# Second phase's x: 32x32 blocks turned by VectorE and a DRAM scratch read back by columns, in place of TensorE transposes

## The chip, the core and the metric

The kernel runs on one core of a Trainium2 chip. The metric is device time in microseconds (us) of one execution. A core has five engines that each work through their own instructions in order and wait for one another by semaphores: TensorE (PE in the profile; PEld is its weight load), VectorE (DVE), ScalarE (ACT), GpSimd (POOL) and SyncE (SP), which here issues all the DMAs ("SPq" is its queue).

## What is computed

An mLSTM attention block, then two MoE-like feed-forward layers, one after the other, on 3072 tokens of width 320 with an inner width of 2048, all in float32:

```
x = attn_out.transpose(0, 2, 1, 3).reshape(B * S, H * D)   # 3072 x 320
x = _moe_ref(x, ...)       # h = x @ w_in; g = h * clip(h + 3, 0, 6) / 6; g @ w_out
return _moe2_ref(x, ...)   # h = x @ w_in; g = max(h, 0) ** 2;           g @ w_out
```

The attention runs in chunks of 64 steps for 4 batches of 768 steps. The change touches only what lies between the first layer's output and the second layer's input.

## The kernel before

**Tiling.** The 3072 tokens are cut into six blocks `j` of 512: 128 steps of each of the 4 batches `i`. `X[j]` is one tile of 128 partitions (the steps) by 4 batches by 320 features. It holds the attention's output, then the first layer's output, then the second layer's, each written over the one before. A layer (`ph` 0 or 1, the first and second phase) works through each block in 16 slots `m`, one for each 128 of the 2048 inner features. Slots are counted through both phases: in phase 0 block 0 has 24 (its first half goes in two halves), every other block 16, so 104 in phase 0 and 96 in phase 1.

**One slot.** `mm_A` (L634) multiplies w_in by x: 8 matmuls into the PSUM tile `hps`. The operand is `xs[ph, j]`, a tile of x turned so that features lie on the partitions, split into a high part (fp32r, entries 0 to 2) and a low part (entries 3, 4 and the upper half of 2). `act1` (ACT) and `act1b` (DVE) make g from it, `act2` (mostly ACT) and `act2b` (DVE) split g into `gh` and `gl`. `mm_B` (L673) multiplies by w_out: 3 matmuls for each batch, added up over the 16 slots of a block in four PSUM tiles `acc0` to `acc3`, of which there is one each. `mm_B` runs LAG = 2 slots behind `mm_A`.

**Between the blocks.** Behind the last slot of a block, `evac` (L685) empties the four `acc` tiles into `X[j]`; in phase 0 four ACT instructions do this (L688) and scale by 1/6. The next block's first `mm_B` writes the same `acc` tiles, so it waits for `evac`. Before a block starts, its x has to be turned: `t_pe` (L609) makes three TensorE transposes of 128x128 for one batch into a PSUM tile `tp`; `t_hi` (L618, usually ACT) copies `tp` into the high part, and `t_lo` (L622, DVE, two instructions, L625 and L627) makes the low part. For phase 1 these three steps stand in slots 13, 10, 7 and 4 ahead of the block, one batch each.

**What sets the order.** All instructions are written out by hand. `FIRST` is a list of steps that run first, with an engine behind "@" where it isn't the usual one; it reaches through the first 40 slots, block 0's `evac` among them. Behind it stand the steps of `moe()`: for every slot `mm_A`, `act1`, `act1b`, the steps hooked at "pe", `mm_B` of two slots ago, `evac`, the steps hooked at "ew" (attention, loads, weight work), `act2`, `act2b`. The attention units are hooked into phase 0 up to slot 84, and the second layer's weights are loaded and split (`w_load`, `w_exp`, `w_bits`, `w_hilo`) from slot 90 on, since they lie in the same SBUF as the first layer's.

Of the kernel before, what the change touches and what calls it, by code (L numbers as in the profile page):

```python
# [8 lines left out]
F32 = mybir.dt.float32  # L9
F32R = mybir.dt.float32r  # L10
# [3 lines left out]
ACTF = mybir.ActivationFunctionType  # L14
ALU = mybir.AluOpType
# [12 lines left out]
TB = 512  # L28
# [93 lines left out]
def kernel(ctx, tc, qk, kn, va, gates, og, w1i, w1o, w2i, w2o, out):  # L122
    nc = tc.nc
    B, NC, D, _, H, _ = qk.shape
    BH = B * H
    S = NC * L
    NT, DM = out.shape
    NG, P, KI3, GC = w1i.shape
    MG = w1o.shape[2]
    NM = NG * MG  # L130
    E0 = 64
    KX = E0 + D
    DV = D + 1
    NPR = S // P
# [16 lines left out]
    xs_p = ctx.enter_context(tc.tile_pool(name="xs", bufs=2))  # L151
    g_p = ctx.enter_context(tc.tile_pool(name="g", bufs=2))
    gh_p = ctx.enter_context(tc.tile_pool(name="gh", bufs=3))
    at2 = ctx.enter_context(tc.tile_pool(name="at2", bufs=2))
    dram = ctx.enter_context(tc.tile_pool(name="dram", bufs=1, space=DRAM))
# [13 lines left out]
    kI = [const.tile([KX, H, D], F32, name=f"kI{i}") for i in range(3)]  # L169
    Z = [[const.tile([KX, H, DV], F32, name=f"Z{b}{i}") for i in range(2)] for b in range(B)]  # L170
    X = [xpool.tile([P, B, DM], F32, name=f"X{p}") for p in range(NPR)]
    Gd = dram.tile([NC, BH, L], F32, name="Gd")

    UL = 4
# [8 lines left out]
    for step in FIRST.split():  # L183
        step, _, eng = step.partition("@")
        if eng:
            name, _, a = step.partition(":")
            ENG[(name, *(int(n) for n in a.split(",")))] = eng

    def on(name, usual, *a):
        return {"v": nc.vector, "g": nc.gpsimd}[ENG.get((name, *a), usual)]  # L190

    def copy(name, *a):
        return nc.vector.tensor_copy if ENG.get((name, *a)) == "v" else nc.scalar.copy
# [13 lines left out]
    gb = pre[:, B, 0:NC1 * P].rearrange("p (c k) -> p c k", k=P)  # L207
    gx, gy = (t[0:BH].rearrange("p b d -> p (b d)") for t in X[NPR - 2:])

# [117 lines left out]
    T = {}  # L327
# [77 lines left out]
    def x_tile(u):  # L405
        if ("X", u) not in T:
            T["X", u] = at2.tile([KX, H, KX], F32, tag="Xm", name="Xm")
        return T["X", u]

# [73 lines left out]
    def at_Y(u):  # L483
        b, c = units[u]
        Xm = T["X", u]
        pool, tag = (ps_acc, "acc0") if u in (1, 3) else (ps_y, "y")
# [41 lines left out]
    def at_n3(u):  # L528
        b, c = units[u]
        yt = T["yt", u]  # L530
        p0 = (c % 2) * L
        xo = X[c // 2][p0:p0 + L, b, :].rearrange("p (h d) -> p h d", d=D)
        on("at_n3", "v", u).tensor_tensor(out=xo, in0=xo, in1=yt[p0:p0 + L], op=ALU.mult)  # L533
# [72 lines left out]
    xs = {}  # L606


    def t_pe(ph, j, i):  # L609
        x = X[j][:, i, :]  # L610
        if (ph, j) not in xs:
            xs[ph, j] = xs_p.tile([P, 5, TB], F32R, tag="xs", name="xs")
        tp = T["tp", ph, j, i] = ps_s.tile([P, 3, P], F32, tag="s", name="tp")

        for k, c0 in enumerate((0, P, KB)):
            nc.tensor.transpose(out=tp[:, k, :], in_=x[:, c0:c0 + P], identity=ident)  # L616

    def t_hi(ph, j, i):  # L618
        n = slice(i * P, i * P + P)
        copy("t_hi", ph, j, i)(out=xs[ph, j][:, 0:3, n], in_=T["tp", ph, j, i])  # L620

    def t_lo(ph, j, i):  # L622
        t, tp = xs[ph, j], T["tp", ph, j, i]
        n = slice(i * P, i * P + P)
        nc.vector.tensor_tensor(  # L625
            out=t[:, 3:5, n], in0=tp[:, 0:2], in1=t[:, 0:2, n].bitcast(F32), op=ALU.subtract)
        nc.vector.tensor_tensor(  # L627
            out=t[0:E0, 2, n], in0=tp[E0:P, 2], in1=t[E0:P, 2, n].bitcast(F32), op=ALU.subtract)

    acc = {}  # L630
# [54 lines left out]
    def evac(s, i):  # L685
        ph, j, m, i0, i1 = slots[s]
        if ph == 0:
            nc.scalar.activation(out=X[j][:, i, :], in_=acc[i], func=ACTF.Copy, scale=1.0 / 6.0)  # L688
        else:
            copy("evac", s, i)(out=X[j][:, i, :], in_=acc[i])  # L690
            r0 = i * S + j * P
            nc.sync.dma_start(out=out[r0:r0 + P, :], in_=X[j][:, i, :])
# [9 lines left out]
    first = {}  # L702
# [8 lines left out]
    at_x2 = (x_q, x_k)  # L711
    at_norm = (at_n1, at_n2, at_n3)
    x_T = (t_pe, t_hi, t_lo)
    w_bits = (w_b1, w_b2)
    w_hilo = (w_hi, w_lo)

# [10 lines left out]
    def at(s, part, f, *a):  # L727
        hooks.setdefault((s, part), []).append((f, *a))
# [5 lines left out]
    LAG = 2  # L734

    def moe():
        for s in range(len(slots) + LAG):
            if s < len(slots):
                seq.append((mm_A, s))
                seq.append((act1, s))  # L740
                seq.append((act1b, s))
            run(s, "pe")
            if s >= LAG:
                ph, j, m, i0, i1 = slots[s - LAG]
                for i in range(i0, i1):
                    seq.append((mm_B, s - LAG, i))
                if m == NM - 1:
                    for i in range(i0, i1):
                        seq.append((evac, s - LAG, i))
            run(s, "ew")  # L750
            if s < len(slots):
                seq.append((act2, s))
                seq.append((act2b, s))
        assert not hooks, list(hooks)
# [5 lines left out]
    for u in range(6, NU):  # L760
        b, c = units[u]
        if c % 2:
            at(at_slot[u] + 3, "pe", x_T, 0, c // 2, b)
    for u in range(UL, NU):
# [13 lines left out]
        at(s, "ew", at_C, u)  # L778
        at(s, "ew", at_norm, u)
    for j in range(NB):  # L780
        for i in range(B):
            at(first[1, j, 0] - 13 + 3 * i, "pe", x_T, 1, j, i)
    s1 = first[0, NB - 1, 0] + 2


# [6 lines left out]
    for p, s in ((4, 45), (5, 45)):  # L792
# [4 lines left out]
    steps = {f.__name__: f for f in (  # L797
        o_load, load_gates, o_sig, at_qk, at_kn, at_va, const_g, const_i, const_m, const_o, const_z, const_k, const_l, gate_m, gate_g, gate_G, gate_b,
        gate_bT, head_rows, at_rg, at_gload, w_pe, qk_split, w_load, w_add, w_mask, w_e, x_q, at_S, at_P, w_exp, x_k,
        w_b1, w_b2, at_Y, at_n1, at_n2, at_n3, at_C, w_hi, w_lo, t_pe, t_hi,  # L800
        t_lo, mm_A, act1, act1b, act2, act2b, mm_B, evac)}
    todo = []
    for step in FIRST.split():
        name, _, a = step.partition("@")[0].partition(":")
# [63 lines left out]
```

## Time and profile before

| what | value |
|---|---|
| median of 3 runs | 838.53 us (838.03 to 838.98) |
| the profiled execution, its own time | 839.09 us |
| its span, first to last instruction | 837.3 us |
| PE busy | 810.1 us, 97% of the span |
| PEld / DVE / ACT / POOL busy | 86% / 65% / 51% / 27% |

The chain of work that ended last is on TensorE for 89% of the span; the matmuls of L640 (`mm_A`) and L681 (`mm_B`) make up 79%. Matmuls are pipelined: one begins before the one ahead has ended, so the duration of one is longer than what it adds to the stream. What it adds is read from the starts in the timeline.

### The profile page before, as it was taken

Reading aid. Unit: us, or ns where it says so; the run is one execution under the profiler, and the core shown is the slowest. Engines: PE = TensorE matmul, PEld = TensorE weight load, DVE = VectorE, ACT = ScalarE, POOL = GpSimd, SP = SyncE. Lnnn points to the kernel's source line nnn. Section 1 sums busy time; section 2 is a strip of 40 time slices with the busy share of each in tenths; the row PEclk is TensorE's granted clock in tenths of the full one; section 3 lists DMA queues with packets and bytes.
Section 4 is the critical chain, followed back from the end, with each engine's and each line's share of the span. In section 5 each row is a group of like instructions: output and inputs, shape, how many; then the busy total and the mean of one; then the engine's idle time right before and its main releaser. Section 6 shows DMA issues by size and latency. Waiting matters only on the chain.

```text
span 837.3 us, 19199 instructions
## 1 busy us (share of the span) xinstructions
PE 810.1 (97%) x7967; PEld 719.9 (86%) x7968; DVE 548.1 (65%) x919; ACT 427.9 (51%) x815; POOL 224.8 (27%) x201
## 2 busy tenths in 40 slices
PE   5798999999999999999999999999999999999998
PEld 3587888889888888888899989989989989999997
DVE  8688998888778788878547788544344344344332
ACT  6778674466565545554346666433333433433433
POOL 5554555353454454453001333100000000000000
PEclk9598999999999999999999999999999999999999
DMA  7955442531433343340034520000000000000000
GB/s 229 294 178 182 122 120 79 117 91 44 119 96 100 85 120 92 104 108 2 2 106 181 187 81 1 1 33 1 32 1 0 32 1 1 32 1 1 32 1 31
DMA packets 28674, 63.59 MB, mean 76 GB/s; under 512 B 4748, under 2 KB 17100, under 8 KB 28588
## 3 DMA queue, kind: packets, MB, share of 16 engines
q1 hardware_dynamic: 28588, 62.38, 25.1%
q8 instruction: 62, 1.02, 0.5%
q14 instruction: 24, 0.20, 0.1%
HBM read 58.36 MB, written 4.00 MB: 74 GB/s over the span
## 4 chain that ended last, share of the span: by engine, by line
PE 89%; ACT 4%; DVE 3%; issue 2%; POOL 1%; DMA 0%; ACTq 0%; POOLq 0%; DVEq 0%; SPq 0%
PE hps L640 40%; PE acc L681 39%; PE Yp L491 4%; PE tp L616 2%; PE Sp L457 2%; PE Sp L449 1%; ACT yt L520 1%; PE Sp L451 1%; PE Wp L372 1%; ACT Xm L421 0%; ACT g L649 0%; ACT qs L433 0%; ACT X L688 0%; PE Sp L464 0%; PE Wp L370 0%
## 5 line engine op out<-in xcount | busy, mean ns | idle before, releaser
L640 PE MATMUL hps<-xs,wi 128*128 128x512 f32 (+1 forms) x1600 | 389.9, 387 | 1.7 <-DVE gl L671 1.0
L681 PE MATMUL acc<-wo,gh 128*128 128x320 f32 x1536 | 348.2, 313 | 0.0
L640 PEld LDWEIGHTS hps<-xs,wi 128*128 128x128 f32 x1600 | 287.5, 190 | 51.9 <-DVE gl L671 1.4
L681 PEld LDWEIGHTS acc<-wo,gh 128*128 128x128 f32 x1536 | 259.1, 188 | 9.9
L681 PE MATMUL acc<-wo,gl 128*128 128x320 f32 x768 | 237.7, 309 | 0.5 <-DVE gl L671 0.5
L671 DVE TENSOR_TENSOR gl<-g,gh 128x512 fp32r<-128x512 f32 x176 | 130.9, 745 | 66.0 <-ACT gh L666 64.7
L661 DVE TENSOR_TENSOR g<-g 128x512 f32<-128x512 f32 x96 | 66.4, 691 | 127.6 <-ACT g L651 127.1
L681 PEld LDWEIGHTS acc<-wo,gl 128*128 128x128 f32 x768 | 144.4, 188 | 1.0 <-DVE gl L671 1.0
L666 ACT CAST gh<-g 128x512 fp32r<-128x512 f32 x169 | 104.5, 619 | 68.0 <-DVE g L661 53.3
L649 ACT ACTIVATE g<-hps,less 128x512 f32<-128x512 f32 (+1 forms) x104 | 68.0, 654 | 136.5 <-PE hps L640 120.9
L651 ACT ACTIVATE g<-hps 128x512 f32<-128x512 f32 x96 | 57.4, 598 | 151.5 <-PE hps L640 151.5
L658 DVE SCALAR_TENSOR_TENSOR g<-g,hps 128x512 f32<-128x512 f32 x80 | 54.7, 685 | 49.0 <-ACT g L649 48.7
L413 POOL TENSOR_TENSOR Xm<-qkt,W 40x512 f32<-40x512 f32 x31 | 40.9, 1321 | 109.1 <-ACT W L403 83.5
L601 POOL TENSOR_TENSOR wi<-wt,wi 128x768 fp32r<-128x768 f32 x14 | 26.5, 1894 | 107.0 <-ACT wi L596 101.7
L379 POOL TENSOR_TENSOR W<-W,bT 104x512 f32<-104x512 f32 x32 | 43.4, 1358 | 15.5 <-DMA W<-Gd 12.4
L491 PEld LDWEIGHTS Yp<-Z,Xm 104*32 104x32 f32 (+1 forms) x3072 | 35.2, 111 | 14.3 <-issue 11.8
L435 DVE SCALAR_TENSOR_TENSOR qs<-qs,less,qkt 120x512 fp32r<-120x512 f32 x52 | 38.0, 773 | 8.5 <-ACT qs L433 8.3
L491 PE MATMUL Yp<-Z,Xm 104*32 104x41 f32 (+1 forms) x3072 | 41.1, 210 | 1.0 <-issue 0.9
L601 POOL TENSOR_TENSOR wo<-wt,wo 128x640 fp32r<-128x640 f32 x15 | 24.8, 1653 | 30.8 <-ACT wo L596 30.7
L533 DVE TENSOR_TENSOR X<-X,yt 64x320 f32<-64x320 f32 x34 | 29.9, 881 | 4.1 <-ACT yt L520 3.1
L616 PE MATMUL tp<-ident,X 128*128 128x128 f32 x144 | 24.7, 282 | 8.0 <-DVE xs L627 5.1
L449 PEld LDWEIGHTS Sp<-qkt 40*64 40x64 f32 x256 | 19.5, 158 | 13.1 <-issue 6.4
(106 smaller groups left out, 703.4 us busy)
## 6 DMA issues: line engine op xcount, KB each, us to landing
qkt<-in_qk SPq DMA_DIRECT2D x74, 160.0 KB
W<-Gd SPq DMA_DIRECT2D x32, 208.0 KB
rwi<-in_w1i SPq DMA_DIRECT2D x8, 768.0 KB
rwi<-in_w2i SPq DMA_DIRECT2D x8, 768.0 KB
rwo<-in_w1o SPq DMA_DIRECT2D x8, 640.0 KB
rwo<-in_w2o SPq DMA_DIRECT2D x8, 640.0 KB
Z<-in_va SPq DMA_DIRECT2D x48, 82.0 KB
kI<-in_kn SPq DMA_DIRECT2D x48, 80.0 KB
```

The lines of the kernel that those rows point to most:

```text
L379: on("w_add", "g", u).tensor_tensor(out=W, in0=W, in1=bT[:, c - NC1, b * H:(b + 1) * H].unsqueeze(2).to_broadcast([KX, H, L]), op=ALU.add)
L491: nc.tensor.matmul(out=Yp[o:e, h, :], lhsT=Xm[:, h, o:e], rhs=Z[b][c % 2][:, h, :], start=True, stop=True)
L601: on("w_lo", "g", ph, i).tensor_tensor(out=w[:, 1], in0=f, in1=w[:, 0].bitcast(F32), op=ALU.subtract)
L616: nc.tensor.transpose(out=tp[:, k, :], in_=x[:, c0:c0 + P], identity=ident)
L640: nc.tensor.matmul(out=h, lhsT=w[:, hl, kk, o:o + P], rhs=t[:, xk, i0 * P:i1 * P], start=(i == 0), stop=(i == len(TERMS) - 1))
L649: nc.scalar.activation(out=g, in_=T["h", s], func=ACTF.Relu, bias=three)
L651: nc.scalar.activation(out=g, in_=T["h", s], func=ACTF.Relu)
L658: nc.vector.scalar_tensor_tensor(out=g, in0=r, scalar=6.0, in1=T["h", s], op0=ALU.min, op1=ALU.mult)
L661: nc.vector.tensor_tensor(out=g, in0=r, in1=r, op=ALU.mult)
L666: copy("act2", s)(out=gh, in_=g)
L671: nc.vector.tensor_tensor(out=gl, in0=g, in1=gh.bitcast(F32), op=ALU.subtract)
L681: nc.tensor.matmul(out=acc[i], lhsT=g[:, n], rhs=w[:, hl, m % MG, :], start=(m == 0 and q == 0), stop=(m == NM - 1 and q == 2))
```

## The change

In phase 0, `evac` is no longer an ACT copy but a DVE `transpose` of the whole `acc[i]`: each 32x32 block of its 128x320 is turned by itself. It is written into `X[j]` seen as 10 pieces of 128 (`x_blocks`), so that a partition holds, for one feature in each group of 32, the steps of all four batches. `x_out` then sends a block to a DRAM scratch `Xd[j]` with features as rows, in four DMAs of 32 partitions each, with runs of 128 floats. `x_in` reads the scratch back with features on the partitions: one DMA for the first 256 features and two for the last 64, which stand in `xs` twice. The tiles take their buffers from two tags of the attention, `qk` and `Xm`.

For phase 1 `t_pe` is gone. `t_hi` is three ACT instructions that read the tiles from `x_in` and scale by 1/6, and `t_lo` three DVE instructions. They stand where they stood. Phase 0's own turns (of the attention's output) stay as they were.

```diff
@@ -169,6 +169,7 @@
     kI = [const.tile([KX, H, D], F32, name=f"kI{i}") for i in range(3)]
     Z = [[const.tile([KX, H, DV], F32, name=f"Z{b}{i}") for i in range(2)] for b in range(B)]
     X = [xpool.tile([P, B, DM], F32, name=f"X{p}") for p in range(NPR)]
+    Xd = [dram.tile([DM, 4, P], F32, name=f"Xd{p}") for p in range(NPR)]
     Gd = dram.tile([NC, BH, L], F32, name="Gd")
 
     UL = 4
@@ -606,6 +607,27 @@
     xs = {}
 
 
+    def x_blocks(j):
+
+
+        return X[j].rearrange("p b d -> p (b d)").rearrange("p (k t) -> p k t", t=P)
+
+    def x_out(j):
+        for r in range(4):
+            nc.sync.dma_start(
+                out=Xd[j].rearrange("(k p) r t -> p k r t", p=32)[:, :, r],
+                in_=x_blocks(j)[32 * r:32 * r + 32])
+
+    def x_in(j):
+        m = at2.tile([P, 2, TB], F32, tag="qk", name="xm", bufs=3)
+        e = at2.tile([P, TB], F32, tag="Xm", name="xe")
+        x = Xd[j].rearrange("d r t -> d (r t)")
+        nc.sync.dma_start(out=m, in_=x[0:2 * P].rearrange("(q p) n -> p q n", p=P))
+        for o in (0, E0):
+            nc.sync.dma_start(out=e[o:o + E0], in_=x[2 * P:])
+        T["xt", j] = (m.rearrange("p q (r i t) -> p q i r t", r=4, i=B),
+                      e.rearrange("p (r i t) -> p i r t", r=4, i=B))
+
     def t_pe(ph, j, i):
         x = X[j][:, i, :]
         if (ph, j) not in xs:
@@ -617,11 +639,31 @@
 
     def t_hi(ph, j, i):
         n = slice(i * P, i * P + P)
+        if ph == 1:
+            m, e = T["xt", j]
+            if i == 0:
+                xs[1, j] = xs_p.tile([P, 5, TB], F32R, tag="xs", name="xs")
+            t = xs[1, j][:, :, n].rearrange("p k (r t) -> p k r t", r=4)
+            for q in range(2):
+                nc.scalar.activation(out=t[:, q], in_=m[:, q, i], func=ACTF.Copy, scale=1.0 / 6.0)
+            nc.scalar.activation(out=t[:, 2], in_=e[:, i], func=ACTF.Copy, scale=1.0 / 6.0)
+            return
         copy("t_hi", ph, j, i)(out=xs[ph, j][:, 0:3, n], in_=T["tp", ph, j, i])
 
     def t_lo(ph, j, i):
+        n = slice(i * P, i * P + P)
+        if ph == 1:
+            m, e = T["xt", j]
+            t = xs[1, j][:, :, n].rearrange("p k (r t) -> p k r t", r=4)
+            for q in range(2):
+                nc.vector.scalar_tensor_tensor(
+                    out=t[:, 3 + q], in0=m[:, q, i], scalar=1.0 / 6.0, in1=t[:, q].bitcast(F32),
+                    op0=ALU.mult, op1=ALU.subtract)
+            nc.vector.scalar_tensor_tensor(
+                out=t[0:E0, 2], in0=e[0:E0, i], scalar=1.0 / 6.0, in1=t[0:E0, 2].bitcast(F32),
+                op0=ALU.mult, op1=ALU.subtract)
+            return
         t, tp = xs[ph, j], T["tp", ph, j, i]
-        n = slice(i * P, i * P + P)
         nc.vector.tensor_tensor(
             out=t[:, 3:5, n], in0=tp[:, 0:2], in1=t[:, 0:2, n].bitcast(F32), op=ALU.subtract)
         nc.vector.tensor_tensor(
@@ -685,7 +727,9 @@
     def evac(s, i):
         ph, j, m, i0, i1 = slots[s]
         if ph == 0:
-            nc.scalar.activation(out=X[j][:, i, :], in_=acc[i], func=ACTF.Copy, scale=1.0 / 6.0)
+            nc.vector.transpose(
+                out=x_blocks(j)[:, :, 32 * i:32 * i + 32],
+                in_=acc[i].rearrange("p (k t) -> p k t", t=32))
         else:
             copy("evac", s, i)(out=X[j][:, i, :], in_=acc[i])
             r0 = i * S + j * P
@@ -711,6 +755,7 @@
     at_x2 = (x_q, x_k)
     at_norm = (at_n1, at_n2, at_n3)
     x_T = (t_pe, t_hi, t_lo)
+    x_split = (t_hi, t_lo)
     w_bits = (w_b1, w_b2)
     w_hilo = (w_hi, w_lo)
 
@@ -778,8 +823,10 @@
         at(s, "ew", at_C, u)
         at(s, "ew", at_norm, u)
     for j in range(NB):
+        at(first[0, j, NM - 1] + LAG + 3, "ew", x_out, j)
+        at(86 if j < 2 else first[1, j, 0] - 18, "ew", x_in, j)
         for i in range(B):
-            at(first[1, j, 0] - 13 + 3 * i, "pe", x_T, 1, j, i)
+            at(first[1, j, 0] - 13 + 3 * i, "pe", x_split, 1, j, i)
     s1 = first[0, NB - 1, 0] + 2
 
 
@@ -797,7 +844,7 @@
     steps = {f.__name__: f for f in (
         o_load, load_gates, o_sig, at_qk, at_kn, at_va, const_g, const_i, const_m, const_o, const_z, const_k, const_l, gate_m, gate_g, gate_G, gate_b,
         gate_bT, head_rows, at_rg, at_gload, w_pe, qk_split, w_load, w_add, w_mask, w_e, x_q, at_S, at_P, w_exp, x_k,
-        w_b1, w_b2, at_Y, at_n1, at_n2, at_n3, at_C, w_hi, w_lo, t_pe, t_hi,
+        w_b1, w_b2, at_Y, at_n1, at_n2, at_n3, at_C, w_hi, w_lo, x_out, x_in, t_pe, t_hi,
         t_lo, mm_A, act1, act1b, act2, act2b, mm_B, evac)}
     todo = []
     for step in FIRST.split():
```

On **DVE** at the end of phase 0's block 1 stood, before (L658 is `act1b`, L435 the attention's `qk_split`, L671 `act2b`, L505 to L523 its normalization):

```order
L671 TENSOR_TENSOR gl<-g,gh 128x512
L658 SCALAR_TENSOR_TENSOR g<-g,hps 128x512
L435 SCALAR_TENSOR_TENSOR qs<-qs,less,qkt 120x512 x2
L671 TENSOR_TENSOR gl<-g,gh 128x512
L658 SCALAR_TENSOR_TENSOR g<-g,hps 128x512
```

and now:

```order
L713 TENSOR_TENSOR gl<-g,gh 128x512
L700 SCALAR_TENSOR_TENSOR g<-g,hps 128x512
L730 STREAM_TRANSPOSE X_110<-acc_2593 128x10x32
L730 STREAM_TRANSPOSE X_110<-acc_2471 128x10x32
L730 STREAM_TRANSPOSE X_110<-acc_2647 128x10x32
L730 STREAM_TRANSPOSE X_110<-acc_2570 128x10x32
L436 SCALAR_TENSOR_TENSOR qs<-qs,less,qkt 120x512 x2
L713 TENSOR_TENSOR gl<-g,gh 128x512
L700 SCALAR_TENSOR_TENSOR g<-g,hps 128x512
```

Four transposes came in between `act1b` and the two instructions of `qk_split`; blocks 2 and 3 end in the same way, and ACT lost four copies there.

On **DVE** at the end of block 0, which `FIRST` orders, stood before (L480 is the attention's `at_P`, L533 its last step, L620 to L627 turn block 1's x for phase 0):

```order
L625 TENSOR_TENSOR xs<-tp,xs 128x2x128
L627 TENSOR_TENSOR xs<-tp,xs 64x128
L505 RECIPROCAL rd<-Yp 64x8
L507 TENSOR_SCALAR rd<-rd 64x8
L523 SCALAR_TENSOR_TENSOR yt<-rd,Yp 64x320
L533 TENSOR_TENSOR X_111<-X_111,yt 64x320
L480 TENSOR_TENSOR Xm<-Sp,W 64x4x64
L658 SCALAR_TENSOR_TENSOR g<-g,hps 128x512
L480 TENSOR_TENSOR Xm<-Sp,W 64x4x64
```

and now:

```order
L730 STREAM_TRANSPOSE X_109<-acc_1268 128x10x32
L651 CAST xs<-tp 128x3x128
L667 TENSOR_TENSOR xs<-tp,xs 128x2x128
L669 TENSOR_TENSOR xs<-tp,xs 64x128
L506 RECIPROCAL rd<-Yp 64x8
L508 TENSOR_SCALAR rd<-rd 64x8
L730 STREAM_TRANSPOSE X_109<-acc_717 128x10x32
L524 SCALAR_TENSOR_TENSOR yt<-rd,Yp 64x320
L534 TENSOR_TENSOR X_111<-X_111,yt 64x320
L481 TENSOR_TENSOR Xm<-Sp,W 64x4x64
L730 STREAM_TRANSPOSE X_109<-acc_805 128x10x32
L700 SCALAR_TENSOR_TENSOR g<-g,hps 128x512
```

Here the four transposes are spread; the first stands six instructions above the rows shown, and the second `at_P` follows below.

On **SP**, around the loads of the second layer's weights (`rwi`, `rwo`), stands now:

```order
L625 DMA xm<-Xd_116 128x2x512
L627 DMA xe<-Xd_116 64x512 x2
L564 DMA rwi_6502<-in_w2i 128x768
L564 DMA rwo_6539<-in_w2o 128x640
L617 DMA Xd_119<-X_113 32x10x128 x4
L564 DMA rwi_6573<-in_w2i 128x768
```

Before, the weight loads followed one another there. The scratch of blocks 0 and 1 is now read ahead of them, block 4 is written between the second and the third, and block 5 behind the sixteenth.

## Rows read from the trace of the kernel before

**Rows 1.** The page: busy time by engine, and the granted clock in 40 slices.
```profile
PE 810.1 (97%) x7967; PEld 719.9 (86%) x7968; DVE 548.1 (65%) x919; ACT 427.9 (51%) x815; POOL 224.8 (27%) x201
...
PEclk9598999999999999999999999999999999999999
```

**Rows 2.** Stretches: length, busy PE, PEld, DVE, ACT, POOL, clock, DMA share, GB/s.
```profile
100.00:200.00 100.00, 99.25 (x1476) 85.49 (x1475) 86.81 (x157) 57.96 (x146) 49.06 (x46) 1.00 0.34 92
200.00:400.00 200.00, 196.53 (x2590) 173.52 (x2589) 160.46 (x271) 111.94 (x191) 94.48 (x85) 1.00 0.34 89
...
500.00:760.00 260.00, 260.00 (x1468) 235.12 (x1467) 123.75 (x190) 105.21 (x186) 10.94 (x6) 1.00 0.03 11
```

**Rows 3.** PE timeline in phase 1: start, duration in us, line, operation, count.
```profile
603.44 2.00 PE L640 MATMUL hps<-xs,wi 128*128 128x512 f32 x8
...
607.03 2.00 PE L640 MATMUL hps<-xs,wi 128*128 128x512 f32 x8
608.88 0.49 PE L616 MATMUL tp<-ident,X 128*128 128x128 f32 x3
...
610.96 2.00 PE L640 MATMUL hps<-xs,wi 128*128 128x512 f32 x8
```

**Rows 4.** Phase 1's turns in the PE timeline: first and last of 24.
```profile
432.36 0.49 PE L616 MATMUL tp<-ident,X 128*128 128x128 f32 x3
...
759.91 0.49 PE L616 MATMUL tp<-ident,X 128*128 128x128 f32 x3
```

**Rows 5.** Line L616 alone: count, nanoseconds min/median/max, first and last start.
```profile
L616 PE MATMUL tp<-ident,X x144: 270/272/473, 31.3 to 760.1; 128*128 128x128 f32 x144
```

**Rows 6.** Groups by shape: count, busy us, mean ns of one, idle before.
```profile
L625 DVE TENSOR_TENSOR xs<-tp,xs 128x256 fp32r<-128x256 f32 x48 | 20.2, 421 | 0.9
...
L620 ACT CAST xs<-tp 128x384 fp32r<-128x384 f32 x42 | 19.9, 473 | 4.6 <-PE tp L616 4.6
...
L627 DVE TENSOR_TENSOR xs<-tp,xs 64x128 fp32r<-64x128 f32 x48 | 14.1, 293 | 0.8
...
L620 DVE CAST xs<-tp 128x384 fp32r<-128x384 f32 x6 | 3.3, 554 | 2.0 <-PE tp L616 2.0
...
L323 DVE STREAM_TRANSPOSE bT<-X 32x256 f32<-32x256 f32 x2 | 0.9, 429 | 0.0
...
L239 ACT CAST identb<-ident 128x128 bf16<-128x128 f32 x1 | 0.3, 298 | 0.0
```

**Rows 7.** DVE timeline, end of block 1; in brackets the idle time before.
```profile
216.27 0.69 DVE L658 SCALAR_TENSOR_TENSOR g<-g,hps 128x512 f32<-128x512 f32 x1 [0.80 <-ACT g L649]
218.71 1.41 DVE L435 SCALAR_TENSOR_TENSOR qs<-qs,less,qkt 120x512 fp32r<-120x512 f32 x2 [1.75 <-ACT qs L433]
```

**Rows 8.** Waits over the whole span: who for whom, total us, times, longest.
```profile
PE Sp L457 <- DVE qs L435: 1.3, 3, 0.4
```

**Rows 9.** DVE timeline at the end of block 0.
```profile
141.81 0.42 DVE L480 TENSOR_TENSOR Xm<-Sp,W 64x256 f32<-64x256 f32 x1 [0.27 <-PE Sp L464]
...
142.87 0.41 DVE L480 TENSOR_TENSOR Xm<-Sp,W 64x256 f32<-64x256 f32 x1
```

**Rows 10.** PE timeline at the end of block 0.
```profile
144.10 0.81 PE L491 MATMUL Yp<-Z,Xm 104*32 104x41 f32 x64
```

**Rows 11.** DVE timeline at the end of block 4.
```profile
428.10 0.69 DVE L671 TENSOR_TENSOR gl<-g,gh 128x512 fp32r<-128x512 f32 x1 [1.26 <-ACT gh L666]
429.74 0.69 DVE L658 SCALAR_TENSOR_TENSOR g<-g,hps 128x512 f32<-128x512 f32 x1 [0.95 <-ACT g L649]
```

**Rows 12.** PE timeline behind block 4: block 5's first matmuls into acc3.
```profile
430.07 0.46 PE L681 MATMUL acc<-wo,gh 128*128 128x320 f32 x2
```

**Rows 13.** SP queue's timeline: third load of the second layer's weights.
```profile
435.04 0.42 SPq L563 DMA_DIRECT2D rwi<-in_w2i  x1
```

**Rows 14.** ACT timeline: the first instruction that reads this load.
```profile
452.53 0.91 ACT L575 ACTIVATE rwi<-rwi 128x768 f32<-128x768 f32 x1
```

**Rows 15.** The page, DMA queues: packets, MB, share of 16 engines.
```profile
q1 hardware_dynamic: 28588, 62.38, 25.1%
```

## The prediction, made before the changed kernel ran

> **What bounds the kernel now.** I read the busy times first, then the stretches, then the PE timeline. TensorE is busy for 810.1 of 837.3 us [rows 1]; what it lacks lies mostly in the first 100 us. From 200 to 400 us it is busy for 196.5 of 200, and from 500 to 760 for 260 of 260 [rows 2]. The granted clock is full (9 tenths or more) from the fifth slice on, that is from 84 us [rows 1]. So behind the first 100 us an instruction taken out of TensorE's stream shortens the run by what it adds to the stream, unless another engine then comes late. The nearest to that is VectorE: 86.8 of 100 us and 160 of 200 in the first phase, but 124 of 260 in the second [rows 2]. So the second phase has room, and the first phase, in which the new `evac` stands, has little.
>
> **The removal, 24 turns of three transposes.** A single transpose lasts 272 ns [rows 5], but that is its passage, not what it adds. The starts tell that [rows 3]: from one `mm_A` to the next it is 607.03 - 603.44 = 3.59 us in a slot without a turn and 610.96 - 607.03 = 3.93 us in a slot with one. A turn costs 0.34 us. Phase 1 has 24 of them, from 432.36 to 759.91 [rows 4], all where PE has no idle time to fill: 24 x 0.34 = **8.2 us out**. Taken at the duration of the row, 72 x 0.272 us would make 19.6 us; the pitch of the slots contradicts that. [...]
>
> **The new evac on VectorE.** The trace has one kind of DVE transpose, 32x256 out of SBUF in 429 ns [rows 6]. For 320 elements that is 429 x 320/256 = 536 ns if all of it grows with the length. From below: a plain DVE copy out of PSUM takes 554 ns for 384 [rows 6], so 462 for 320. I take 0.50 us, the middle, since fixed parts of 429 ns don't grow; four make 2.0 us. Whether 128 partitions and a PSUM source cost more no row shows; that is a rival below. What the four push back differs by place.
>
> - Blocks 1 to 3. Behind `act1b` (ends at 216.96) VectorE idles 1.75 us for ACT's copy for `qk_split` (L435), which on ACT stands behind the four old copies [rows 7]. Now the copy is early and the four transposes fill that gap, 2.0 in place of 1.75. `qk_split` comes 0.25 us later. PE already waits for `qk_split` here, three times and at most 0.4 us each [rows 8], so nothing covers it: 3 x 0.25 = 0.8 us back.
> - Block 0. All four stand ahead of the second `at_P` (L480, ends at 143.28), and the only idle time on the way is 0.27 us [rows 9]. It would end at 143.28 + 2.0 - 0.27 = 145.0. PE's `at_Y` that needs it starts at 144.10 [rows 10]. **0.9 us back**; from 0 (other slack that I don't see) to 2.1 (all four at 0.54).
> - Block 4. VectorE idles 1.26 us ahead of `act2b` at 428.10, that is from 426.84 on [rows 11]. The transposes take 426.84 to 428.84, `act2b` ends at 429.5 in place of 428.8, and the next instruction starts at 429.74 anyway, behind 0.95 us of idle [rows 11]. The next block's `mm_B` into acc3 starts at 430.07 [rows 12], and acc3 is empty at 428.8. Nothing. Block 5 has the same shape, with no attention behind it: nothing.
>
> Together 0.8 + 0.9 = **1.7 us back**, from 0 (0.46 each: 1.84 for four against 1.75 of idle, and slack at block 0) to 3 x (4 x 0.54 - 1.75) + 2.1 = 3.3 us.
>
> **The other work, at nothing.** ACT loses 24 copies. `t_hi` is three instructions for one of 473 ns; the nearest row is a 128x128 copy of 298 ns, so 0.9 us, 0.4 more. `t_lo` is three for two of 421 + 293 = 714 ns; at 293 each (the row of 64x128 in two operands) that is 0.88, 0.2 more [rows 6]. Neither engine is over half busy in the second phase [rows 2], and `mm_B` asks for `gl` only two slots, 7.2 us, after `mm_A`, which covers this; without that cover it would be 24 x 0.6 = 14 us. Nor does `t_hi` wait for PE any more.
>
> The DMAs all go to SP. `x_out` stands three slots behind `evac`; behind it queue the attention's loads, whose tiles rotate over three units of two slots, so they lead by some 20 us, while four issues at 0.42 [rows 13] cost 1.7. The tightest place is block 4's `x_out`, which now precedes the third weight load. That load is issued at 435.04 [rows 13] and first read at 452.53 [rows 14]: 17.5 us. The mean packet took 0.251 x 16 x 837.3 us/28588 = 118 ns for 2.2 KB [rows 15]; four DMAs of 320 runs are 1280 packets of 512 bytes, at most 1280 x 118/16 ns = 9.4 us, and the load's own 768 KB some 2.7 us by the same rate. It still lands 5 us early. `x_in` stands five slots (18 us) ahead of the first `t_hi` and moves 768 KB, like one weight load. Both are hidden; the price of being late is in the rivals.
>
> **The sum.** The profiled execution took 839.09 us, of which the span is 837.3. 839.1 - 8.2 + 1.7 = 832.6. The median of the runs is 0.56 us below the profiled execution, so for the median **832.0 us**. The bounds of the unknown costs give 830.3 to 833.6. [...]
>
> **The rivals.**
> - *All of VectorE's new work shows.* In the first phase it is the second bound, and what block 0 delays need not be made good. Then the 16 transposes of blocks 0 to 3 cost 16 x 0.5 = 8.0 us: 838.5 - 8.2 + 8.0 = 838.3, no change. For it: 86.8% busy around block 0 [rows 2]. Against it: 1.75 us of idle just where the four go [rows 7].
> - *The transposes are dear; slower.* If one out of PSUM on 128 partitions costs twice the row's 536 ns, 1.07 us, four take 4.3. Blocks 1 to 3 lose 4.3 - 1.75 = 2.55 each, block 0 4.3 - 0.27 - 0.8 = 3.2. Behind block 4 acc3 is empty at 426.84 + 4.3 = 431.1 against 430.07 [rows 12], 1.0 lost, block 5 alike: 12.9 in all, 838.5 - 8.2 + 12.9 = 843.2. It turns slower where 3 x (4d - 1.75) + (4d - 1.1) + 2 x (4d - 3.2) passes 8.2 us, at d = 0.87 us. For it: no row has this form. Against it: DVE copies take 554 ns out of PSUM on 128 partitions, no more than their length asks.
> - *x or weights come late.* If the 512-byte packets cost twice the mean, `x_out` of block 4 takes 18.8 us and the third weight load lands 4 us late (18.8 + 2.7 - 17.5); ACT stands still for that and everything behind it: about 836.
> - *The transposes cost what they last.* 19.6 us out: 838.5 - 19.6 + 1.7 = 820.6. Against it stand [rows 3].
>
> **How the numbers follow.** Faster, same and slower are parted at 0.2% (1.7 us), about what a measurement of this kernel can tell from no change: 836.85 and 840.2. The forecast, 829.5 to 834.5 with the unknowns: 0.70. All of VectorE's work shows (837 to 840): 0.10. Dear transposes: 0.08, slower. Late transfers: 0.04, half of it faster, half slower. The longer transposes: 0.03, faster. Between forecast and no change (834.5 to 836.8), a part of VectorE's work showing: 0.05, faster. Faster 0.70 + 0.02 + 0.03 + 0.05 = 0.80; same 0.10; slower 0.10. The range needs 8 in 10 and takes the forecast, the case between and the lower half of the first rival: 829.5 to 838.0.
>
> **What would show it.** In the changed profile: no L616 behind 430 us, and every slot of phase 1 at 3.59 us; STREAM_TRANSPOSE out of `acc` at 0.46 to 0.54 us; the `Sp` matmuls behind blocks 1 to 3 waiting for `qk_split` 0.6 to 0.7 us in place of 0.4; an idle time of about 0.9 us ahead of `at_Y` behind block 0; no wait of ACT for `xm` or of any engine for the weights. The forecast is wrong if a transpose takes over 0.87 us, if PE's idle time between 100 and 430 us grows by over 4 us, or if slots of the second phase get longer.

## The result, and the profile after

The changed kernel takes 830.47 us (median of 6 runs, 828.84 to 831.9) and the kernel before, in the same runs, 838.79 us. The ratio is 0.9899 with a 95% interval of 0.9885 to 0.9913: 1.0% faster, 8.3 us. The time forecast was 832.0 us with a range of 829.5 to 838.0, so the direction and the range held, and the time came out 1.5 us below the forecast. The profiled execution took 829.99 us, with a span of 828.2.

The page of the changed kernel, busy times by engine, granted clock in 40 slices, and the SP queue's transfers (packets, MB, share of 16 engines), to be read beside [rows 1, 15]:

```profile
PE 802.1 (97%) x7896; PEld 713.4 (86%) x7896; DVE 552.3 (67%) x967; ACT 424.6 (51%) x839; POOL 226.3 (27%) x201
...
PEclk9598999999999999999999999999999999999999
...
q1 hardware_dynamic: 39244, 71.03, 29.4%
```

PE has 8.0 us less to do and VectorE 4.2 us more. The queue carries 10,656 packets more; the granted clock is what it was. The stretches (length, busy PE, PEld, DVE, ACT, POOL, clock, DMA share, GB/s), beside [rows 2]:

```profile
100.00:200.00 100.00, 99.42 (x1478) 85.80 (x1477) 86.33 (x162) 56.27 (x142) 49.40 (x46) 1.00 0.36 98
200.00:400.00 200.00, 197.58 (x2594) 174.32 (x2593) 166.61 (x283) 107.54 (x179) 94.78 (x85) 1.00 0.40 103
500.00:760.00 260.00, 260.00 (x1451) 235.80 (x1450) 123.23 (x212) 111.93 (x229) 11.50 (x6) 1.00 0.06 20
```

In the second phase PE is still without a gap, so it still sets the pace there. In the stretch from 200 to 400 us, where VectorE took over the new work, VectorE is busy for 166.6 instead of 160.5 us, and PE stands still for 2.4 instead of 3.5 us. More work on VectorE went with less waiting on PE. The forecast had this the other way round. Around block 0, from 100 to 200 us, VectorE isn't busier than before (86.3 against 86.8) although it evicts there too.

PE's timeline in phase 1 (start, duration, line, operation, count), beside [rows 3]:

```profile
598.21 2.00 PE L682 MATMUL hps<-xs,wi 128*128 128x512 f32 x8
600.05 0.45 PE L723 MATMUL acc<-wo,gh 128*128 128x320 f32 x2
...
601.80 2.00 PE L682 MATMUL hps<-xs,wi 128*128 128x512 f32 x8
...
605.40 2.00 PE L682 MATMUL hps<-xs,wi 128*128 128x512 f32 x8
```

From one `mm_A` to the next it is 3.59 and 3.60 us, in every slot, where a slot with a turn had 3.93. (`mm_B`, from 600.05 to the next `mm_A` at 601.80, takes 1.75 us; that number is needed below.)

**Where the 8.9 us lie.** The first 210 us differ between executions of one and the same kernel by more than a microsecond (the matmul named next starts at 212.2 and at 209.68 us in the two executions of the kernel with the transposes behind `qk_split`, below), so I laid the traces on each other at one matmul that stands in all of them, `at_Y` at 210.45 us before and 210.29 after, with the same 0.87 us of idle time ahead of it. Its line before, and in the changed kernel:

```profile
210.45 0.80 PE L491 MATMUL Yp<-Z,Xm 104*32 104x41 f32 x64 [0.87 <-issue]
```

```profile
210.29 0.80 PE L492 MATMUL Yp<-Z,Xm 104*32 104x41 f32 x64 [0.87 <-issue]
```

From there to the end of the span it is 626.85 us before and 617.91 after: 8.94 us less. The first `mm_A` behind the end of each 512-token block divides this (starts read in the two PE timelines):

| stretch | before, us | after, us | difference | turns gone |
|---|---|---|---|---|
| marker to end of block 1 | 6.65 | 6.66 | 0.0 | 0 |
| block 1 to 2 | 71.90 | 71.41 | -0.5 | 0 |
| 2 to 3 | 70.66 | 70.32 | -0.3 | 0 |
| 3 to 4 | 67.26 | 67.05 | -0.2 | 0 |
| 4 to 5 | 58.84 | 57.50 | -1.3 | 4 |
| 5 to the end | 351.5 | 345.0 | -6.6 | 20 |

The turns are 7.9 us, 0.33 each. The other 1.0 us is a gain in the first phase, where the forecast had a loss of 0.8. In PE's timeline of the changed kernel one sees where it comes from; these are the `Sp` matmuls behind blocks 1, 2 and 3 and, second in the list, the one of another unit at 246.5 us (in brackets the idle time ahead and who ended it):

```profile
219.87 0.62 PE L458 MATMUL Sp<-qs 120*64 120x64 f32 x8 [0.18 <-PE Yp L492]
...
246.51 0.62 PE L458 MATMUL Sp<-qs 120*64 120x64 f32 x8 [0.84 <-DVE qs L436]
...
291.33 0.62 PE L458 MATMUL Sp<-qs 120*64 120x64 f32 x8 [0.24 <-DVE qs L436]
...
361.65 0.62 PE L458 MATMUL Sp<-qs 120*64 120x64 f32 x8 [0.24 <-DVE qs L436]
```

The three waits of up to 0.4 us in [rows 8] have become 0.18 to 0.24. The one at 246.5 us was 1.31 us in the trace before and is 0.84 here, but in the ten profiled executions of the experiments it was 0.82 to 0.84 in six and near 1.3 in four, and the two repeats of the changed kernel show both. It goes either way, and is no part of what the change does. Of its 0.47 us only about half reaches the end of block 2: from block 1 to 2 the three traces of the changed kernel take 71.39, 71.41 (both with the short wait) and 71.65 us (with the long one), against 71.90 before with the long one. So of the 1.0 us about 0.8 is the gain of the change in the first phase.

VectorE's timeline at the end of block 1, beside [rows 7]:

```profile
216.12 0.69 DVE L700 SCALAR_TENSOR_TENSOR g<-g,hps 128x512 f32<-128x512 f32 x1 [0.81 <-ACT g L691]
216.72 1.70 DVE L730 STREAM_TRANSPOSE X<-acc 128x320 f32<-128x320 f32 x4
218.35 1.37 DVE L436 SCALAR_TENSOR_TENSOR qs<-qs,less,qkt 120x512 fp32r<-120x512 f32 x2
```

Four transposes take 1.70 us, and no bracket stands ahead of `qk_split` (L436): it starts when VectorE is free, not when ACT's copy is there. It starts 2.23 us after the start of `act1b` (218.35 - 216.12), where it was 2.44 before [rows 7]. All 24 transposes, then the new work around the scratch by shape (count, busy us, mean ns of one, idle before), which answers to [rows 6]:

```profile
L730 DVE STREAM_TRANSPOSE X<-acc x24: 468/473/517, 136.4 to 484.6; 128x320 f32<-128x320 f32 x24
```

```profile
L648 ACT ACTIVATE xs<-xm 128x128 fp32r<-128x128 f32 x48 | 12.0, 302 | 0.0
...
L649 ACT ACTIVATE xs<-xe 128x128 fp32r<-128x128 f32 x24 | 7.2, 299 | 0.0
...
L662 DVE SCALAR_TENSOR_TENSOR xs<-xe,xs 64x128 fp32r<-64x128 f32 x24 | 6.7, 277 | 0.0
```

A single transpose is recorded with 473 ns in the median; in a row they start some 0.41 us apart ((1.70 - 0.473)/3). The new `t_hi` costs three times 0.30 us as forecast, `t_lo` a little less than forecast, and the 0.0 at the end of each group says that neither ACT nor VectorE ever stood waiting for x to come back from DRAM.

### The profile page after: what moved, and what is told of

It reads as the page before. It is cut to its first block, busy times and chain, and to the rows that moved or that the text cites. A ratio compares the mean times of both kernels' runs of the same rounds, so it can differ in the third digit from the quotient of the medians.

```text
span 828.2 us, 19221 instructions
## 1 busy us (share of the span) xinstructions
PE 802.1 (97%) x7896; PEld 713.4 (86%) x7896; DVE 552.3 (67%) x967; ACT 424.6 (51%) x839; POOL 226.3 (27%) x201
## 4 chain that ended last, share of the span: by engine, by line
PE 90%; DVE 4%; ACT 2%; issue 2%; DMA 1%; POOL 0%; SPq 0%; ACTq 0%; DVEq 0%; POOLq 0%
PE hps L682 41%; PE acc L723 39%; PE Yp L492 4%; PE Sp L458 2%; PE tp L638 1%; PE Sp L450 1%; DVE qs L436 1%; PE Sp L452 1%; ACT yt L521 1%; DMA W<-Gd 1%; PE Wp L373 1%; PE Sp L465 0%; PE Wp L371 0%; DMA qkt<-in_qk 0%; DVE X L730 0%
## 5 line engine op out<-in xcount | busy, mean ns | idle before, releaser
L414 POOL TENSOR_TENSOR Xm<-qkt,W 40x512 f32<-40x512 f32 x31 | 40.7, 1313 | 106.7 <-ACT W L404 82.2
L380 POOL TENSOR_TENSOR W<-W,bT 104x512 f32<-104x512 f32 x32 | 44.1, 1378 | 16.8 <-DMA W<-Gd 16.4
L436 DVE SCALAR_TENSOR_TENSOR qs<-qs,less,qkt 120x512 fp32r<-120x512 f32 x52 | 37.9, 769 | 3.3 <-ACT qs L434 2.9
L450 PE MATMUL Sp<-qkt 40*64 40x64 f32 x256 | 22.0, 248 | 8.7 <-DMA qkt<-in_qk 5.3
```

What stands on the lines that cost most here:

```text
L436: nc.vector.scalar_tensor_tensor(out=y[0:KS, i], in0=y[0:KS, i].bitcast(F32), scalar=less[0:KS, i:i + 1], in1=x[0:KS, i], op0=ALU.mult, op ...
L450: nc.tensor.matmul(out=Sp[0:L, h, :], lhsT=qkt[E0:KX, 1, h, :], rhs=q, start=True, stop=True)
```

## The experiments

All times are medians beside runs of the kernel before on the same chip (838.8, 838.6 and 838.55 us in the three sets). "From the marker" is the length from the matmul at about 210 us to the end of the span in the profiled execution.

**The changed kernel again, in the first and the third set.** No edit.

> The changed kernel once more, on the chip of the runs beside it, as the base for them. 8.0 to 9.0 us under the kernel before.

Measured: 830.28 us, ratio 0.9895 (0.9874 to 0.9915); 618.09 us from the marker.

> The changed kernel again, beside the run that moves the evacuations: 8 to 9 us under the kernel before.

Measured: 829.57 us, ratio 0.9892 (0.9873 to 0.9910); 617.87 us from the marker. The gain is the same on each chip, and the marker lengths of three executions (617.91, 618.09, 617.87) agree within 0.2 us, so differences of half a microsecond can be read from them.

**The turns back.** Everything of the change stays, and PE gets its 24 x 3 transposes of phase 1 again, into a PSUM tile that nothing reads.

```
     if ph == 1:
+        tp = ps_s.tile([P, 3, P], F32, tag="s", name="tp")
+        for k, c0 in enumerate((0, P, KB)):
+            nc.tensor.transpose(out=tp[:, k, :], in_=X[j][:, i, c0:c0 + P], identity=ident)
         m, e = T["xt", j]
```

> The changed kernel with the 24 turns of three transposes put back into TensorE's stream; nothing reads what they write. Theory 1 (the turns were worth 0.34 us each and the rest of the change gains a little): 7.9 to 8.2 us above the changed kernel, some 0.5 to 1 us under the kernel before, slots with a turn 3.93 us long. Theory 2 (the turns were worth more, up to 10 us, and the new evacuation gave 1.7 back): 10 us above the changed kernel, 1.7 above the kernel before.

Measured: 837.67 us, ratio 0.9989 (0.9973 to 1.0004): 0.9 us are left of the lead of 8.3, and the interval can't tell that from nothing. From the marker it is 626.21 us, 8.1 more than in the repeat of the changed kernel with which it shares the longer wait near 247 us (618.09). That is 0.34 us for each of the 24. PE's timeline has the old pitch again:

```profile
605.07 2.00 PE L685 MATMUL hps<-xs,wi 128*128 128x512 f32 x8
...
608.66 2.00 PE L685 MATMUL hps<-xs,wi 128*128 128x512 f32 x8
610.50 0.49 PE L645 MATMUL tp<-ident,X 128*128 128x128 f32 x3
...
612.58 2.00 PE L685 MATMUL hps<-xs,wi 128*128 128x512 f32 x8
```

3.59 us without a turn, 3.92 with one. So the gain is the removed transposes, at the price the pitch gave, and the rest of the change costs nothing in sum; in the trace it gains some 0.6 us (626.21 against 626.85, both with the longer wait).

**The eviction on VectorE alone, as a plain copy.** The kernel before, with only the engine of phase 0's `evac` changed; the transposes on PE stay.

```
-            nc.scalar.activation(...)
+            nc.vector.tensor_scalar(
+                out=X[j][:, i, :], in0=acc[i],
+                scalar1=1.0 / 6.0, scalar2=None, op0=ALU.mult)
```

> The kernel before, with one part of the change alone: the 24 first-phase evacuations as a scaled VectorE copy in place of the ScalarE copy; the turns on TensorE stay. Theory 1 (the VectorE work at the block ends fits into idle time and into instructions that stand waiting anyway, and ScalarE's copy for qk_split comes earlier): 0.5 to 1.2 us under the kernel before, and the three waits of Sp for qk_split fall from 0.43 to about 0.2 us each. Theory 2 (the forecast's: the block ends give back time): 1 to 1.7 us above the kernel before, and these waits grow to 0.6 to 0.7.

Measured: 838.03 us, ratio 0.9988 (0.9974 to 1.0002); 625.87 us from the marker, 0.98 less than before, of which about 0.24 is the wait near 247 us that goes either way. (The interval of the whole runs includes no change at all; the gain is read from the trace.) The copy as VectorE ran it, and PE's first and third `Sp` behind a block:

```profile
L688 DVE TENSOR_SCALAR X<-acc x24: 473/479/492, 137.9 to 487.4; 128x320 f32<-128x320 f32 x24
```

```profile
221.30 0.62 PE L457 MATMUL Sp<-qs 120*64 120x64 f32 x8 [0.18 <-PE Yp L491]
...
363.08 0.62 PE L457 MATMUL Sp<-qs 120*64 120x64 f32 x8 [0.23 <-DVE qs L435]
```

A copy of this size out of PSUM lasts 479 ns, a transpose 473: turning the blocks costs VectorE nothing over the eviction. And the waits have fallen to the same 0.18 and 0.23 as in the changed kernel. So the small gain of the first phase comes from the eviction's change of engine, not from the transpose or the scratch.

**Every transpose twice.** The changed kernel with each of the 24 evictions done two times, to find what happens when the idle time is used up.

```
-        nc.vector.transpose(...)
+        for _ in range(2):
+            nc.vector.transpose(...)
```

> The changed kernel with every evacuation done twice: 24 VectorE transposes more, about 0.41 us each. Theory 1 (the cover at blocks 1 to 3 is used up by the first four, at blocks 4 and 5 there is room for eight): 3 x 1.65 us at blocks 1 to 3, about 1 at block 0, nothing at blocks 4 and 5: 6 us above the changed kernel. If VectorE's work showed everywhere: 24 x 0.41 = 9.8 us. If there were more cover than the idle time shows: under 2 us.

Measured: 849.26 us, ratio 1.0121 (1.0099 to 1.0142), 19.0 us more than the changed kernel in this set. None of the three numbers expected held. VectorE, PE and POOL at the end of block 1 of this kernel, then the stretches behind blocks 1, 2 and 3 (columns as above):

```profile
218.49 3.90 DVE L731 STREAM_TRANSPOSE X<-acc 128x320 f32<-128x320 f32 x8
222.32 2.38 DVE L436 SCALAR_TENSOR_TENSOR qs<-qs,less,qkt 120x512 fp32r<-120x512 f32 x2
```

```profile
224.85 0.68 PE L458 MATMUL Sp<-qs 120*64 120x64 f32 x8 [3.39 <-DVE qs L436]
225.34 0.88 PE L723 MATMUL acc<-wo,gh 128*128 128x320 f32 x2
...
228.69 1.56 PE L682 MATMUL hps<-xs,wi 128*128 128x512 f32 x6
```

```profile
222.70 1.45 POOL L414 TENSOR_TENSOR Xm<-qkt,W 40x512 f32<-40x512 f32 x1 [3.99 <-ACT W L404]
```

```profile
225.00:230.00 5.00, 5.00 (x26) 4.78 (x26) 3.90 (x8) 0.62 (x1) 2.39 (x3) 0.66 0.64 167
230.00:235.00 5.00, 5.00 (x88) 4.20 (x87) 2.70 (x4) 2.75 (x4) 0.00 (x0) 1.00 0.57 145
...
301.00:306.00 5.00, 4.67 (x22) 4.61 (x23) 4.38 (x9) 0.62 (x1) 2.88 (x3) 0.50 0.39 118
306.00:311.00 5.00, 5.00 (x25) 4.37 (x24) 1.62 (x3) 2.14 (x3) 0.00 (x0) 0.88 0.72 188
...
377.50:382.50 5.00, 4.96 (x25) 4.61 (x26) 4.09 (x8) 0.62 (x1) 2.59 (x3) 0.66 0.59 149
```

Three things come on top of each other. The eight transposes last 2.2 us longer than the four, where 1.65 were expected: in this row they start 0.49 us apart ((3.90 - 0.473)/7), not 0.41. `qk_split`, which stands behind them on VectorE, now falls beside POOL's L414 and takes 2.38 us in place of 1.37. PE therefore stands still for 3.39 us; and behind that wait the granted clock of the stretch is 0.66, and `mm_B` takes 3.35 us (225.34 to 228.69) in place of 1.75. The wait comes at all three blocks (3.39, 3.45, 3.44 us), and the low clock behind each, 0.66 over 5 us, 0.50 and then 0.88, 0.66. Reckoned as 5 us times what is missing to 1, that is 1.7 + 2.5 + 0.6 + 1.7 = 6.5 us; PE's starts behind the three waits, laid on those of the repeat of the changed kernel, give 1.6, 2.7 and 1.6, or 5.9. From the marker the kernel takes 635.44 us, 17.35 more than that repeat, which has the same long wait near 247 us: 3 x 3.2 us more of waiting and 6 of clock make 15.6, and three short waits of PE for acc behind blocks 4 and 5 lie in the rest. What is left of the 19.0 us lies at block 0: from `mm_A` at 121.34 us (121.47 in the repeat) to the marker it is 90.72 us here and 88.93 in the repeat.

POOL's part can be read from all twelve traces of this case: `qk_split` takes 1.37 to 1.42 us where POOL is busy for 0.28 us of it or less, and 1.87 to 2.69 where POOL is busy for 1.26 us of it or more, the three at the block ends of this kernel among them.

**The four transposes behind the split.** If the order on VectorE is what the first phase pays for, then giving `qk_split` precedence must take the three waits away.

```
+                late = ph == 0 and 1 <= j <= 3
-                if m == NM - 1:
+                if m == NM - 1 and not late:
                     for i in range(i0, i1):
                         seq.append((evac, s - LAG, i))
             run(s, "ew")
+            if s >= LAG and m == NM - 1 and late:
+                for i in range(i0, i1):
+                    seq.append((evac, s - LAG, i))
```

> The changed kernel with the evacuations of blocks 1 to 3 moved behind the two VectorE instructions of qk_split. Theory 1: the three waits of Sp (0.18 to 0.24 us) go, the accumulators are still empty in time: 0.6 us under the changed kernel. Rival: the transposes, now later, hold back act2b or the accumulators: the same or up to 1 us above.

Measured: 828.85 us, ratio 0.9883 (0.9864 to 0.9903); 617.17 us from the marker, 0.74 less than the changed kernel with the same 0.84 us of wait near 247 us. VectorE and PE at the end of block 1:

```profile
218.99 1.41 DVE L436 SCALAR_TENSOR_TENSOR qs<-qs,less,qkt 120x512 fp32r<-120x512 f32 x2 [0.25 <-ACT qs L434]
220.32 1.70 DVE L730 STREAM_TRANSPOSE X<-acc 128x320 f32<-128x320 f32 x4
```

```profile
221.55 0.65 PE L458 MATMUL Sp<-qs 120*64 120x64 f32 x8
```

Now `qk_split` waits for ACT's copy again (0.25 us in its bracket) and `Sp` has no bracket: PE doesn't wait, at any of the three blocks.

> The changed kernel with the evacuations of blocks 1 to 3 behind qk_split once more, for a narrower interval: 0.7 us under the changed kernel, 9 us under the kernel before.

Measured: 829.18 us, ratio 0.9888 (0.9868 to 0.9908), against 829.57 for the changed kernel in the same set; 617.12 us from the marker against 617.87. The traces show 0.7 us twice, but between the medians (1.4 and 0.4 us) that can't be told from nothing.

**Twice, and behind the split.** The two edits above together. If what stands in line behind the transposes decides, most of the 19 us must go, though VectorE does the same work.

> The same 24 extra transposes as in the run with every evacuation done twice, but in blocks 1 to 3 all eight stand behind the two instructions of qk_split. Theory (what counts is what stands in line behind the transposes, not VectorE's total work): Sp no longer waits for qk_split, the granted clock stays full, TensorE waits some 0.6 to 1 us a block for the accumulators instead; with 1.6 us at block 0 and 0.3 to 0.6 at blocks 4 and 5 the run is 4 to 6 us above the changed kernel. Rival (VectorE's total work counts): as before, 19 us above the changed kernel.

Measured: 836.91 us, ratio 0.9982 (0.9968 to 0.9997), 7.3 us more than the changed kernel in this set in place of 19. No wait for `qk_split` is left behind the blocks; PE waits for the acc tiles instead, here behind block 1:

```profile
222.44 0.45 PE L723 MATMUL acc<-wo,gh 128*128 128x320 f32 x2
...
223.30 0.53 PE L723 MATMUL acc<-wo,gh 128*128 128x320 f32 x2 [0.26 <-DVE X L731]
...
224.24 0.53 PE L723 MATMUL acc<-wo,gh 128*128 128x320 f32 x2 [0.28 <-DVE X L731]
```

There are nine such waits. Each shows 0.26 to 0.28 us of idle time but moves the starts apart by more: 0.86 and 0.94 us between neighbours that stood 0.44 apart without it, so 0.42 to 0.50 each, some 4 us for nine. From the marker it is 622.10 us, 5.0 more than with single transposes in this order (617.12). The other 2.2 lie at block 0, where the order is as it was: from `mm_A` at 121.38 us to the marker it is 90.72 us again, against 88.55 with single transposes. The order was worth 13.3 us behind the marker (635.44 to 622.10), some 0.2 of it the wait near 247 us: with `qk_split` ahead there is no long wait of PE, and no low clock (1.00 in each stretch from 210 to 530 us).

**The read of x later.** Blocks 2 to 5 of x are read back four slots later, behind the output's transfers on SP.

```
-        at(86 if j < 2 else first[1, j, 0] - 18, "ew", x_in, j)
+        at(86 if j < 2 else first[1, j, 0] - 14, "ew", x_in, j)
```

> The changed kernel with the reading back of blocks 2 to 5 put behind the output DMAs of two blocks ago, one slot ahead of the first t_hi: the lead falls from tens of us to about 4. If the read lands within 4 us or the two slots between mm_A and mm_B cover what is missing: the same time within 0.3 us, with ScalarE waiting a little for xm. If the cover is too small: TensorE waits once per block, 1 us or more each, 4 us or more in all.

Measured: 830.0 us, ratio 0.9899 (0.9883 to 0.9914); 618.16 us from the marker (the repeat of the changed kernel: 618.09). SP's queue and ACT at block 3:

```profile
598.80 0.45 SPq L625 DMA_DIRECT2D xm<-Xd  x1
599.34 1.09 SPq L627 DMA_DIRECT2D xe<-Xd  x2
```

```profile
603.68 0.50 ACT L648 ACTIVATE xs<-xm 128x128 fp32r<-128x128 f32 x2
604.08 0.30 ACT L649 ACTIVATE xs<-xe 128x128 fp32r<-128x128 f32 x1
```

ACT's first reads have no bracket: 768 KB issued from 598.80 on were there at 603.68, 4.9 us later. In the changed kernel SP runs ahead of the slots and issues this read at 542.04, 62 us before its first use at 604.40, so the lead that the change gives it isn't used up by far.

**Only one block through the scratch.** The changed kernel writes, reads and splits block 0 alone, and all six blocks of phase 1 multiply with it; this leaves out five sixths of the work on x.

```
     for j in range(NB):
+        if j > 0:
+            continue
         at(first[0, j, NM - 1] + LAG + 3, "ew", x_out, j)
...
-        t, w = xs[ph, j], Wt[ph, 2 * (m // MG)]
+        t, w = xs[ph, j * (1 - ph)], Wt[ph, 2 * (m // MG)]
```

> The changed kernel with the scratch, the reading back and t_hi and t_lo for block 0 alone; the second phase's other blocks multiply block 0's x, so the 5 x 7 DMAs and the 60 ScalarE and 60 VectorE instructions of blocks 1 to 5 are left out. Theory 1 (all of it is hidden): the same as the changed kernel within 0.3 us. Rival (the transfers or the split cost something): 1 us or more under it.

Measured: 829.58 us, ratio 0.9891 (0.9874 to 0.9907); 617.64 us from the marker against 617.91. 35 DMAs and 120 instructions of ACT and VectorE less are worth some 0.3 us in the trace, and the medians can't tell that from nothing. But for that the way through DRAM is hidden.

## Why the prediction was right, and where it was not

The forecast was a net gain of 6.5 us, 8.2 out and 1.7 back. Measured are 8.3 by the medians (7.3 to 9.6 by the interval) and 8.9 from the marker in the traces. The direction and the larger term were understood; the smaller term had the wrong sign, and the stated range was wide enough for that.

**The removal: right.** 8.2 us were forecast from the pitch of the slots [rows 3]; the traces show 7.9 between the two kernels and 8.1 when the turns are put back. The rival that took a transpose at its recorded duration [rows 5] asked for 19.6 us and fell.

**The 1.7 us back: wrong, in size and in sign.** This is the step that failed: blocks 1 to 3 gained some 0.8 us, and block 0 lost nothing. Its two terms were wrong for different reasons. (Two of its bounds don't follow from its own working either: four transposes of 0.46 against 1.75 us of idle time leave 3 x 0.09 = 0.3 us and not 0, and four of 0.54 at block 0 give 2.16 - 0.27 - 0.82 = 1.1 us and not 2.1.)

- *Blocks 1 to 3, 0.8 us.* Four transposes were put at 2.0 us against 1.75 us of idle time. They take 1.70, since in a row they start 0.41 us apart; the recorded 473 ns lay inside my bounds, but multiplying a duration by four is the mistake that the sum avoided for PE's transposes and made here. The second half of the error: `qk_split` had been bound by ACT's copy, which the change made earlier, so its start could move forward as well as back. The waits went from 0.43 to 0.18 to 0.24 us in place of the 0.6 to 0.7 forecast. The plain copy on VectorE shows the same, so it is the change of engine that did it.
- *Block 0, 0.9 us.* The four transposes stood where they were expected, ahead of the second `at_P` (L481 now), which ends at 143.92; the forecast had it at 145.0. PE's `at_Y` starts at 144.24 with no idle time ahead of it. Nothing was lost: from the `mm_A` at 121.60 us before and 121.73 after to the marker it is 88.85 and 88.56 us. The missing microsecond shows in a small instruction. VectorE and POOL there, of the kernel before:

```profile
138.91 1.18 DVE L507 TENSOR_SCALAR rd<-rd 64x8 int32<-64x8 int32 x1
```

```profile
138.78 1.29 POOL L413 TENSOR_TENSOR Xm<-qkt,W 40x512 f32<-40x512 f32 x1 [0.49 <-POOL X L533]
```

and of the changed kernel:

```profile
139.73 0.50 DVE L508 TENSOR_SCALAR rd<-rd 64x8 int32<-64x8 int32 x1
...
143.52 0.40 DVE L481 TENSOR_TENSOR Xm<-Sp,W 64x256 f32<-64x256 f32 x1
```

```profile
138.91 1.30 POOL L414 TENSOR_TENSOR Xm<-qkt,W 40x512 f32<-40x512 f32 x1
```

Here the instruction is booked with 1.18 and 0.50 us, and in both kernels it ends 0.02 us after POOL's (140.09 and 140.07; 140.23 and 140.21). With doubled transposes it does so again (141.48 and 141.45). All executions of this line say the same: of 48 in the trace before, 28 start while POOL is idle and take 0.16 to 0.17 us, and the 20 that start beside a POOL instruction all end 0.02 to 0.03 us after it; in the changed kernel it is 29 and 19, without an exception. So about 1.0 of the 1.18 us was standing behind POOL, booked as busy time, and transposes that push L507 back use that time. I had read it as work and counted only the 0.27 us of marked idle time as room. That the instruction ends with POOL's is shown by the traces; that this alone made up for the transposes at block 0 isn't, since no run took POOL's instruction away.

**Blocks 4 and 5, and acc: right.** No wait for an acc tile in the changed kernel. The doubled transposes show how far it was from one: then the tiles are late, by three waits of 0.27 us behind blocks 4 and 5 and, with the transposes behind `qk_split`, by six more behind blocks 1 to 3.

**The other work at nothing: right.** `t_hi`, `t_lo`, the scratch and its reads: leaving out five sixths of it gains some 0.3 us in the trace, and reading four slots later costs nothing. Block 4's `x_out` did push the third weight load back, from 435.04 to 435.95 us, and its first reader started without a wait. The four issues took longer than the 1.7 us I had put down for them (2.35), which found the same cover.

**The rivals.** *All of VectorE's work shows* fell: PE waits less in the first phase, not more. *Dear transposes* fell at 473 ns, well below the 0.87 us from which it decides; but the mechanism is real, and the doubled transposes show its price: by its formula 3.90 us in a row cost 10.7 us, and 19 were measured. I had charged only the delay itself; the slower `qk_split` beside POOL (2.38 us in place of 1.37 at block 1) and the clock behind a long wait of PE (0.66 over 5 us there) came on top. *Late transfers* and *transposes cost what they last* fell.

**What stays open.** Why the wait near 247 us takes now 0.84 and now 1.3 us; it moves the length of a profiled execution by about a quarter of a microsecond. All twelve traces show what it goes with: where `qk_split` ahead of it takes 2.19 us, POOL's L380 beside it takes 1.60 and the wait is short, and where `qk_split` takes 2.68 or 2.69, L380 takes 1.04 and the wait is long. What decides between the two isn't shown. Open too is whether the order with the transposes behind `qk_split` is faster as measured by whole runs.

## What to carry to other kernels

Price an instruction that you add to or take from a busy in-order stream by the distance of its neighbours' starts, with and without it, on every engine: here 0.11 us for a transpose of 272 ns on PE, and 0.41 us for one of 473 ns on VectorE. When a step changes engines, ask for both queues what now comes earlier and what now comes later; what stands in line behind the step, not the engine's total of busy time, decided between 7 and 19 us here. A cover that is nearly used up (1.70 of 1.75 us) is worth a second look at the order: when doubled transposes overran it here, each wait of 3.4 us was followed by a lower clock (0.66, 0.50 and 0.66 over the next 5 us), which cost another 1.6 to 2.7 us.

## What the runs showed of the hardware that was not expected

- A 128x320 f32 transpose in 32x32 blocks out of PSUM lasts as long on VectorE as a plain copy of that size: 473 and 479 ns.
- A wait of PE of 3.4 us was followed each time by matmuls at a lower granted clock (0.66, 0.50 and 0.66 over the next 5 us), and `mm_B` took 3.35 us in place of 1.75 behind block 1. Behind 170 us, the six waits of 0.43 to 1.31 us in the trace before and the six of 0.18 to 0.87 us in that of the changed kernel were each followed by 5 us at a clock of 1.00, though a stop of 0.27 us within `mm_B` moved the starts by 0.42 to 0.50 with doubled transposes behind `qk_split`.
- `qk_split` took 1.37 to 1.42 us with POOL busy for 0.28 us of it or less, and 1.87 to 2.69 with POOL busy for 1.26 us or more; a 64x8 instruction of 0.16 us that started beside a POOL instruction was booked with 0.2 to 1.2 us, as busy time, and ended 0.02 to 0.03 us after it, 20 times out of 20 in the kernel before and 19 out of 19 in the changed one.
